# A written order of 1,403 steps replaced by another one, in a fused linear-attention and gated-MLP kernel

## The chip, the cores and the metric

The kernel runs on one core of a Trainium2 chip. The metric is the device time of one execution in microseconds (us), less is better. A core has a matrix engine (PE, which takes its weights through a load stream, PEld), a vector engine (DVE), a scalar engine (ACT), a general engine (POOL), a queue (SP) from which nearly all transfers are issued here, and 16 DMA engines. Each engine takes its instructions in the order in which they were written and waits on semaphores for the others.

## What is computed

For each of 4 batches and 8 heads of width 48, over 768 positions: a state of 48 x 48 decays and collects outer products, and the query reads it. The result x (768 x 384 for each batch) goes through a gated layer.

```python
f = 1.0 / (1.0 + np.exp(-f_logit))
for t in range(S):
    state = f[:, :, t, :, None] * state + np.einsum('bhd,bhe->bhde', k[:, :, t], v[:, :, t])
    y[:, :, t] = np.einsum('bhd,bhde->bhe', q[:, :, t], state)
...
h = np.maximum(x @ w_in, 0.0)
...
    conv_out += conv_w[k][None, None, :] * hp[:, k:k + S, :]
gate = 1.0 / (1.0 + np.exp(-conv_out))
return (h * gate @ w_out).astype(np.float32)
```

w_in is 384 x 1024, w_out 1024 x 384, the convolution has three taps along the positions. The weights come as 64-bit numbers and are made into float32 on the core.

## The kernel before

**Attention.** Positions are cut into 24 chunks of 128 (6 for each batch, numbered 0 to 23). Each chunk goes through: loads F (gates), L (k), M (q), V (v), all issued by SP; x (ACT: exp and ln of the gates); G (sums of them: for chunks 0 to 5 PE, tile pl, L292; later a DVE scan, L297); p (ACT: two exponentials, fi and fd); K (DVE: k scaled, L317 and L320); Q (q scaled, L324: on DVE for chunks 0 to 4, then on POOL); t (POOL: one column of fd). Then the four steps with PE work:

- a, the scores: PE products of k and q into the one PSUM tile pa (L345, from chunk 9 on L351), then a masked copy on DVE (am, L355 and L358).
- k, the transposes: four PE transposes of k into ptk (L330), then a copy on ACT (kp, L333). ptk shares its one PSUM buffer ("s") with pk.
- s, the state: PE products of kp and v into pk (L371, later L376); DVE adds the old state (st, L384); POOL multiplies by the decay (L386).
- y, the values: a first PE visit multiplies scores and v, a second one multiplies q and the state of the chunk before (both py, L398); ACT copies the result into xT (L426) and DVE writes the remainder that the copy's rounding left (L428). xT is thus held as a high and a low half.

**The layer.** A unit is half a batch (384 positions, numbers 0 to 7). Step m*u.f* is one 128-wide slice f of the hidden layer of unit u: three PE visits of three matmuls each (ph, L454: high weights with both halves of xT, low weights with the high half), then relu (L457) and one tap on ACT (L462), two taps on DVE (L464, L466). Step j is tanh on ACT (L473) and the product on DVE (L475). Step r*b.m* is one 128-position slice of the output: the product is split into high and low (gh on ACT, L493; gl on DVE, L495), four PE visits of six matmuls (po, L507), a copy on ACT (L512) and the store. pl, ph and po share three PSUM buffers. The steps c, I, J, H, O, P, S load the weights, make them float32 (POOL, ACT, DVE: L179 to L189) and split them (L192, L195). z, b, h are small ones.

**The order.** Each step is a generator that issues one or a few instructions and yields. `ORDER` (from L26) is a written list of step names; a name that stands there n times is resumed n times. The loop at L573 resumes them one after the other. Nothing else sets the order of any engine's instructions, and a buffer is reused in the order in which the list releases it.

```python
for e in ORDER.split():
    next(todo[e], None)
```

Of the kernel before, what the change touches and what calls it, by code (L numbers as in the profile page):

```python
# [36 lines left out]
P1 j0.2 S5 P2 m1.0 m1.0 p8 S0 F12 Q7 j0.0 a7 h1.0 L9 m1.1 s6 K8 S5 L10 s6 m0.7 Q8 m1.0 a7 y6 k8 P1 P1 m1.2 m0.5 m0.7
m1.3 k8 j0.2 P1 V9 m1.5 m0.6 h1.2 m1.2 m1.2 m0.4 p9 m1.5 m1.3 s7 P2 K9 P4 s7 P1 P4 j0.4 a8 y6 y6 m1.2 P4 P4 S2 m1.3 P1
F13 k9 p9 y7 k9 y7 m1.2 V8 m0.6 m1.4 j0.4 s7 m1.5 a8 m1.7 y7 m1.4 y7 m1.3 m1.4 F14 y8 m1.1 V11 m0.6 m0.7 y8 S1 x12 m1.3
a9 M10 t8 h1.4 L11 m1.5 S2 m1.2 Q9 P4 m1.4 G10 P4 O7 m1.5 P6 P6 a9 s8 j0.6 m1.4 j0.6 y8 S4 y8 h1.6 P6 m1.7 P7 m1.7 m1.2  # L40
s8 P7 m1.6 s8 m1.7 m1.6 M12 m1.6 m1.3 m2.3 p10 m2.3 p10 m2.2 a9 m2.3 m1.6 r0.0 m2.5 m2.2 m1.4 j1.2 L12 K10 r0.1 j1.2
m2.5 m2.2 P6 P6 S1 m2.5 k10 y9 k10 m2.3 m1.5 Q10 S4 a10 s9 m1.7 y9 M13 a10 m2.4 P6 h2.2 P7 P7 S6 m2.2 P7 m2.4 M11 r0.0
t9 r0.0 m1.5 m1.4 S6 j1.4 P7 j1.4 S7 m2.4 S7 m2.5 r0.0 r0.1 m1.1 m1.0 r0.0 y9 r0.0 r0.0 m1.6 r0.1 G11 m1.1 p11 m1.6 r0.1
r0.1 p11 m1.0 m1.0 L13 r0.1 h2.4 t11 m1.6 t10 m1.7 s9 m1.7 m2.4 m2.1 a10 y9 m2.7 r0.1 m2.7 m2.6 r0.2 m2.6 j1.6 j1.0 F15
r0.0 m2.1 r0.2 V10 j1.6 s9 x12 m2.1 Q11 j1.0 K11 G12 m2.7 m2.6 h2.6 m2.4 F17 r0.2 s10 m2.1 r0.5 y10 y10 a11 r0.5 p12 F16
r0.2 m2.6 s10 m2.7 m2.0 h2.0 y10 m2.0 m2.5 m2.0 G14 r0.2 r0.2 x15 m2.4 G13 K12 x15 r0.2 p13 G15 K13 M14 p12 a11 m2.5 p13
s10 r0.5 r0.5 m2.0 r0.1 r0.2 r0.4 m2.2 r0.5 r0.5 V12 m2.1 y10 p14 m2.2 r0.2 r0.4 m2.3 r0.5 m2.2 V13 L14 t12 t13 Q12 Q13
k13 y11 k13 y11 a12 k12 K14 m2.0 m2.6 p15 m2.1 y11 m2.3 r0.2 r0.3 m2.3 m2.1 r0.4 r0.4 y11 m2.5 m2.4 M15 r0.4 r0.4 r0.4
p15 m3.3 r0.4 j2.2 m3.3 m3.2 m3.0 m3.3 k12 a12 V14 a13 y12 m2.0 L15 s12 r0.3 m2.0 j2.4 L16 r0.5 j2.2 m3.0 m3.2 j2.0 m3.0
h3.2 G16 j2.0 a13 y12 m3.2 m2.6 p14 t14 s12 K15 m3.3 m3.1 m3.2 h3.0 m3.1 Q14 j2.4 r0.3 h3.4 r0.3 p16 m2.6 m3.0 m3.1 K16  # L50
F19 m2.7 r0.3 r0.3 m3.1 m2.7 y12 m3.1 L17 m3.4 V16 k14 m2.7 Q15 m3.3 G17 r0.3 r0.3 m3.4 F18 m3.4 m3.7 F20 y13 k14 s13
y13 j2.6 s13 m3.4 y13 y13 a14 k15 p17 j2.6 t15 m3.5 m3.5 r1.0 m3.0 m3.5 K17 m3.5 s13 h3.6 a14 m3.7 m3.7 M18 m3.6 k15
m3.1 m3.6 m3.5 m3.5 s14 y14 L18 y14 M16 r1.0 m3.7 m3.4 s14 a15 r1.1 m3.0 k16 m3.0 p16 m3.4 y14 r1.1 x18 V15 p17 m3.2 x18
m3.6 m3.4 V17 r1.0 r1.0 Q16 L19 V20 y14 a15 m3.6 M17 m3.2 m3.6 m3.7 r1.0 r1.1 Q17 G18 r1.0 r1.0 s14 m3.1 t16 r1.1 r1.1
m3.5 m3.3 m3.3 r1.2 k16 r1.1 m4.4 j3.4 p18 m3.7 r1.1 m3.7 r1.1 s15 y15 y15 M19 m3.6 m3.6 a16 j3.0 j3.4 h4.4 m4.4 s15
m3.2 L23 y15 j3.6 y15 j3.0 m4.4 j3.6 m4.4 j3.2 F22 a16 m4.5 h4.6 m4.6 j3.2 m4.5 m4.6 s15 m4.6 K18 r1.5 m4.7 m4.5 F21 s16
r1.2 r1.2 y16 m4.5 y16 h4.2 y16 p18 a17 s16 r1.2 k18 F23 a17 m4.6 x21 G19 m4.1 m4.5 m4.5 y16 m4.7 m4.7 m4.6 m4.1 m4.1
x21 r1.2 r1.2 m4.1 p19 r1.2 k18 t17 r1.2 Q18 m4.5 m4.6 m4.6 r1.5 K19 s16 m4.7 L20 m4.4 y17 y17 r1.0 m4.4 a18 k19 m4.4
G20 m4.3 r1.2 y17 r1.3 t18 m4.2 p19 p20 m4.2 k19 m4.2 m4.3 a18 m4.7 y17 h4.0 m4.0 j4.4 m4.0 m4.0 m4.7 t19 m4.7 Q19 m4.2
r1.3 m4.3 j4.6 j4.4 m4.1 r1.2 m4.3 V18 m4.1 K20 m4.2 G21 m4.0 m4.0 m4.0 a19 y18 m4.0 M20 s18 j4.6 r1.5 r1.5 y18 y18 r1.5  # L60
r1.5 m4.2 m4.1 s18 h5.4 m5.7 r1.5 j4.0 r1.3 h5.6 m5.6 m5.7 r1.3 m5.7 m4.3 a19 m5.6 m4.2 r1.4 j4.0 r1.3 r1.3 p20 m4.3
m5.7 m4.3 m5.6 r1.3 m5.0 G22 j4.2 m5.3 p21 p21 m5.0 G23 h5.0 m5.0 V19 j4.2 m5.3 s19 y19 s19 y19 Q20 m5.0 r2.1 r1.4 a20
k20 m5.3 r1.5 m5.6 k20 r1.4 m5.0 m5.7 m5.6 L21 h5.2 L22 m5.3 m5.7 K21 r1.4 m5.5 r2.1 M22 m5.5 m5.4 M21 r1.4 y19 r1.4
m5.5 m5.4 r1.4 m5.4 m5.5 a20 m5.4 m5.7 m5.4 V23 t20 m5.2 y19 r2.1 m5.1 m5.6 s19 m5.1 m5.5 t21 r1.4 m5.3 m5.2 m5.1 m5.2
Q21 p23 m5.6 p23 m5.5 K23 k21 m5.1 m5.4 m5.4 y20 k21 s20 V21 m5.5 m5.0 m5.1 r2.0 m5.2 r2.0 m5.0 p22 y20 a21 r2.1 p22
r2.1 m5.1 m5.2 r1.3 y20 m5.3 j5.6 y20 r2.1 t22 m5.2 m5.2 r2.0 r2.0 m5.1 r2.1 m5.3 m6.5 j5.0 r2.0 r2.2 Q22 j5.2 j5.6 r2.0
# [12 lines left out]
"""


# [646 lines left out]
```

## Time and profile before

| | |
|---|---|
| median of 3 runs | 305.28 us (304.31 to 307.17) |
| profiled execution, its own time | 305.0 us |
| its span, first to last instruction | 303.3 us |
| PE busy | 294.2 us (97%), 3747 matmuls and as many weight loads |
| DVE / ACT / POOL busy | 251.3 / 220.5 / 85.3 us |
| transferred | 35.67 MB |
| granted TensorE clock | full from the first slices on |

The span is 1.7 us shorter than the execution's time: that much lies around it. Below, the page's part 1 gives each engine's busy time; the windows give it by stretch; the list of waits says who waited for whom; the chain of waits follows the work that ended last, and where PE stands in it without a break, the length of a piece is what a block of matmuls cost behind the one ahead of it; the timeline shows single instructions.

### The profile page before, as it was taken

Reading aid. Unit: us, or ns where it says so; the run is one execution under the profiler, and the core shown is the slowest. Engines: PE = TensorE matmul, PEld = TensorE weight load, DVE = VectorE, ACT = ScalarE, POOL = GpSimd, SP = SyncE. Lnnn points to the kernel's source line nnn. Section 1 sums busy time; section 2 is a strip of 40 time slices with the busy share of each in tenths; the row PEclk is TensorE's granted clock in tenths of the full one; section 3 lists DMA queues with packets and bytes.
Section 4 is the critical chain, followed back from the end, with each engine's and each line's share of the span. In section 5 each row is a group of like instructions: output and inputs, shape, how many; then the busy total and the mean of one; then the engine's idle time right before and its main releaser. Section 6 shows DMA issues by size and latency. Waiting matters only on the chain.

```text
span 303.3 us, 8894 instructions
## 1 busy us (share of the span) xinstructions
PE 294.2 (97%) x3747; PEld 273.5 (90%) x3747; DVE 251.3 (83%) x380; ACT 220.5 (73%) x422; POOL 85.3 (28%) x107
## 2 busy tenths in 40 slices
...
GB/s 230 396 385 391 403 191 39 56 333 135 2 72 161 101 59 61 220 72 224 102 37 166 64 124 2 195 2 84 3 30 89 2 28 26 28 1 2 79 54 55
DMA packets 19374, 35.67 MB, mean 118 GB/s; under 512 B 2156, under 2 KB 9092, under 8 KB 19332
## 3 DMA queue, kind: packets, MB, share of 16 engines
...
## 4 chain that ended last, share of the span: by engine, by line
PE 75%; DVE 7%; POOL 3%; issue 1%; ACT 1%; POOLq 0%
PE po L507 31%; PE ph L454 28%; PE py L398 8%; PE pa L351 3%; PE ptk L330 2%; DVE g L466 2%; PE pk L376 2%; DVE g L464 2%; DVE g L475 1%; POOL st L386 1%; PE pa L345 1%; DVE am L358 1%; PE pk L371 1%; POOL q L324 1%; DVE gl L495 1%
## 5 line engine op out<-in xcount | busy, mean ns | idle before, releaser
L454 PE MATMUL ph<-xT,wih 128*128 128x384 f32 x384 | 99.6, 340 | 0.0
L454 PEld LDWEIGHTS ph<-xT,wih 128*128 128x128 f32 x384 | 68.3, 188 | 1.0 <-issue 0.2
L507 PE MATMUL po<-woh,gh 128*128 128x384 f32 x192 | 64.7, 337 | 0.0
L454 PE MATMUL ph<-xT,wil 128*128 128x384 f32 x192 | 64.3, 335 | 0.0
L507 PE MATMUL po<-wol,gh 128*128 128x384 f32 x192 | 64.2, 334 | 0.0
L507 PE MATMUL po<-woh,gl 128*128 128x384 f32 x192 | 64.2, 334 | 0.0
L464 DVE SCALAR_TENSOR_TENSOR g<-hb,cw,g 128x384 f32<-128x384 f32 (+1 forms) x64 | 42.2, 667 | 13.0 <-ACT g L462 12.9
L466 DVE SCALAR_TENSOR_TENSOR g<-hb,cw,g 128x384 f32<-128x384 f32 (+1 forms) x64 | 40.5, 649 | 0.7
L457 ACT ACTIVATE hb<-ph 128x384 f32<-128x384 f32 x64 | 30.7, 487 | 11.4 <-PE ph L454 10.8
L495 DVE TENSOR_TENSOR gl<-g,gh 128x1024 fp32r<-128x1024 f32 (+4 forms) x34 | 30.4, 908 | 9.6 <-ACT gh L493 9.6
L462 ACT ACTIVATE g<-hb,cw 128x384 f32<-128x384 f32 (+1 forms) x64 | 38.0, 614 | 0.3
L507 PEld LDWEIGHTS po<-woh,gh 128*128 128x128 f32 x192 | 36.0, 188 | 0.5 <-issue 0.2
L324 POOL TENSOR_TENSOR q<-q,fd 128x512 f32<-128x512 f32 x19 | 26.9, 1419 | 33.0 <-ACT fd L307 24.3
L507 PEld LDWEIGHTS po<-wol,gh 128*128 128x128 f32 x192 | 36.0, 188 | 0.0
L507 PEld LDWEIGHTS po<-woh,gl 128*128 128x128 f32 x192 | 36.0, 188 | 0.0
L454 PEld LDWEIGHTS ph<-xT,wil 128*128 128x128 f32 x192 | 36.0, 188 | 0.0
L493 ACT CAST gh<-g 128x1024 fp32r<-128x1024 f32 (+4 forms) x34 | 26.4, 800 | 12.7 <-PE po L507 8.8
L386 POOL TENSOR_TENSOR st<-st,ft_all 128x256 f32<-128x256 f32 x16 | 20.8, 1301 | 51.7 <-DVE st L384 51.7
L475 DVE SCALAR_TENSOR_TENSOR g<-g,hb 128x768 f32<-128x768 f32 (+1 forms) x32 | 30.1, 952 | 3.7 <-ACT g L473 3.7
L512 ACT COPY ob<-po 128x384 f32<-128x384 f32 x24 | 11.3, 474 | 29.7 <-PE po L507 27.1
L473 ACT ACTIVATE g<-g 128x768 f32<-128x768 f32 (+1 forms) x32 | 26.7, 846 | 3.9 <-DVE g L466 3.8
L312 POOL COPY ft_all<-fd 128x4 f32<-128x4 f32 x24 | 12.7, 537 | 56.5 <-ACT fd L307 56.5
...
## 6 DMA issues: line engine op xcount, KB each, us to landing
k<-in_k_dram SPq DMA_DIRECT2D x24, 256.0 KB, 4.4
q<-in_q_dram SPq DMA_DIRECT2D x24, 256.0 KB, 4.3
...
fb<-in_f_logit_dram SPq DMA_DIRECT2D x18, 256.0 KB, 4.3
...
wos<-in_moe_w_out_dram SPq DMA_DIRECT2D x8, 384.0 KB, 5.6
...
```

Source lines behind the costliest of these rows:

```text
L324: (nc.vector if n < QV else nc.gpsimd).tensor_tensor(raw["q", n], raw["q", n], fds[n][1], ALU.mult)
L398: nc.tensor.matmul(py[G * p:G * p + G, t, :], lhs, rhs, start=start, stop=stop)
L454: nc.tensor.matmul(ph, w, xts[b, hf][:, t, xl, :], start=(k == 0), stop=(k == 3 * KT - 1))
L457: nc.scalar.activation(hb[:, 2:HS + 2], ph, AF.Relu, scale=0.5)
L462: nc.scalar.activation(cv, hb[:, 1:n + 1], AF.Copy, scale=cw[:, 1, f:f + 1])
L464: nc.vector.scalar_tensor_tensor(cv, hb[:, 2:n + 2], cw[:, 2, f:f + 1], cv, ALU.mult, ALU.add)
L466: nc.vector.scalar_tensor_tensor(cv, hb[:, 0:n], cw[:, 0, f:f + 1], cv, ALU.mult, ALU.add)
L473: nc.scalar.activation(cv, cv, AF.Tanh)
L475: nc.vector.scalar_tensor_tensor(cv, cv, 1.0, h_b[:, fp:fp + 2, 1:n + 1], ALU.add, ALU.mult)
L493: nc.scalar.copy(hi, g[:, f:f + k])
L495: nc.vector.tensor_tensor(lo, g[:, f:f + k], hi.bitcast(F32), ALU.subtract)
L507: nc.tensor.matmul(po, g[:, f, :], w, start=(i == 0), stop=(i == 3 * NF - 1))
```

## The change

`ORDER` is written anew. The same 1,403 resumptions stand in it, each step keeps its own sequence, and every engine gets the same instructions with the same operands; only their places change, on PE, DVE, ACT, POOL and on SP's queue. Three lines of each list, where the chunks 3 to 5 are at work:

```diff
...
-s2 P3 H2.1 m0.3 m0.3 k3 t3 P3 K4 a3 J1.1 G6 m0.3 t4 m0.1 m0.1 y3 m0.1 P3 J1.1 y3 P3 m0.3 P0 p5 h0.4 s3 a4 y3 V6 P3 P0 p5
-x8 s3 x8 V4 O5 K5 H0.1 F9 m0.0 O2 a4 m0.0 k4 m0.2 m0.0 P5 Q5 P5 m0.1 k4 m0.2 M6 m0.7 S3 m0.0 m0.1 H1.1 P0 P0 p6 p6 y3 P0
-s3 S3 m0.4 F10 H2.1 m0.2 m0.0 a5 s4 y4 x9 m0.2 y4 P0 P2 H1.1 O4 P2 Q6 y4 G8 O6 a5 L8 m0.7 m0.5 M8 P5 m0.2 P5 s4 m0.7 t6
...
+m0.3 J1.1 O0 p5 F9 m0.3 J1.1 J1.1 V4 Q4 m0.3 K5 J1.1 m0.1 p5 m0.1 s3 P0 O2 G6 s3 P3 P3 m0.3 y3 H1.1 y3 a4 H2.1 y3 k4
+m0.0 x8 L6 s3 P0 H1.1 m0.2 V5 H0.1 y3 m0.2 k4 a4 m0.0 V6 m0.0 P0 p6 m0.2 P3 s4 Q5 h0.4 a5 H0.1 F11 t5 P0 P0 m0.2 y4 y4
+m0.1 m0.0 O5 x8 m0.5 m0.4 P3 H2.1 L9 m0.1 P0 M8 s4 F10 P5 S3 K6 m0.2 t4 P5 m0.0 O7 m0.2 m0.1 P5 y4 m0.4 p6 m0.5 x9 m0.5
...
```

PE's 405 visits (a visit is what one resumption gives PE) stand in 175 stretches of one kind in the old list and in 162 in the new one. How often a kind follows another, counted from the two lists:

| visit, and the one ahead of it | old | new |
|---|---|---|
| ph or po behind pa, pk or py | 12 | 10 |
| ph or po behind ptk | 13 | 14 |
| ph behind po, and po behind ph | 35 | 22 |
| ptk behind ph or po | 6 | 4 |
| pk behind the first visit of py | 5 | 9 |
| first visit of py behind pk (chunk 9 on) | 7 | 3 |
| pa behind the second visit of py | 15 | 9 |
| pa behind pk | 2 | 5 |
| first visit of py behind pa | 3 | 11 |

Other places that are spoken of below:

- POOL: the old list puts one half of P0's conversion, both halves of P5's, t4 and Q5 ahead of the product of the state of chunk 3 (s3); the new one puts them behind it.
- PE: the transposes k4 stand behind two visits of m0.0 in the old list, directly behind the scores a4 in the new one. The set of PE visits ahead of the first visit of m1.1 is the same in both, and so it is ahead of the first visit of r0.1.
- DVE: ahead of the remainder for chunk 2 (y2) the same instructions stand in both lists; ahead of that for chunk 5 (y5) the same but for one (a tap of m0.3 in the old list, the split S0 in the new one); ahead of r0.1's low half the same.
- SP: ahead of the load L7 the new list also has L9, M7, O7, O1 and V5.

## Rows read from the trace of the kernel before

**Rows 1.** The page, part 1: busy us (share of the span) and instructions.

```profile
PE 294.2 (97%) x3747; PEld 273.5 (90%) x3747; DVE 251.3 (83%) x380; ACT 220.5 (73%) x422; POOL 85.3 (28%) x107
```

**Rows 2.** Windows: stretch, length; PE, PEld, DVE, ACT, POOL busy; clock; DMA.

```profile
20.00:30.00 10.00, 9.72 (x179) 8.69 (x172) 10.00 (x17) 9.58 (x23) 5.10 (x6) 1.00 1.02 385
28.00:60.00 32.00, 30.90 (x422) 27.41 (x421) 31.61 (x48) 29.41 (x59) 20.89 (x22) 1.00 0.51 187
```

**Rows 3.** Waits of PE: us in total, times, longest.

```profile
PE py L398 <- POOL st L386: 1.1, 1, 1.1
```

**Rows 4.** The chain of waits: start us, us, what (number of matmuls).

```profile
81.34 0.44 PE ptk L330 x4
81.78 1.01 PE py L398 x32
82.79 0.45 PE pk L376 x32
83.24 0.60 PE py L398 x24
83.83 0.81 PE pa L351 x24
84.65 1.26 PE ph L454 x6
...
99.43 0.58 PE pk L376 x32
100.02 1.47 PE py L398 x56
...
104.10 8.32 PE po L507 x48
...
115.28 0.60 PE ptk L330 x4
```

**Rows 5.** Timeline of POOL: start us, us, line, operation, tiles, shapes.

```profile
34.76 0.71 POOL L181 TENSOR_SCALAR mswo<-mswo 128x384 f32<-128x384 f32 x1
...
38.23 0.89 POOL L181 TENSOR_SCALAR mswo<-mswo 128x384 f32<-128x384 f32 x1
39.08 4.27 POOL L386 TENSOR_TENSOR st<-st,ft_all 128x256 f32<-128x256 f32 x1
...
44.54 1.61 POOL L324 TENSOR_TENSOR q<-q,fd 128x512 f32<-128x512 f32 x1
...
46.72 0.61 POOL L386 TENSOR_TENSOR st<-st,ft_all 128x256 f32<-128x256 f32 x1
```

**Rows 6.** Timeline of PE around two waits and two first visits.

```profile
41.23 1.08 PE L398 MATMUL py<-am,v 128*32 128x128 f32 x32
43.41 0.80 PE L398 MATMUL py<-q,st 128*32 128x128 f32 x24 [1.10 <-POOL st L386]
...
53.10 0.59 PE L454 MATMUL ph<-xT,wih 128*128 128x384 f32 x2
...
90.43 0.33 PE L507 MATMUL po<-woh,gh 128*128 128x384 f32 x1
```

**Rows 7.** Timeline of DVE at the instructions that PE waits for.

```profile
35.02 0.41 DVE L384 TENSOR_TENSOR st<-pk,st 128x256 f32<-128x256 f32 x1
...
44.90 1.80 DVE L317 TENSOR_TENSOR k<-k,fi 128x512 f32<-128x512 f32 x1
...
49.85 0.69 DVE L317 TENSOR_TENSOR k<-k,fi 128x512 f32<-128x512 f32 x1
...
52.29 0.56 DVE L428 TENSOR_TENSOR xT<-py,xT 128x384 fp32r<-128x384 f32 x1 [0.22 <-ACT xT L426]
...
88.76 1.22 DVE L495 TENSOR_TENSOR gl<-g,gh 128x1024 fp32r<-128x1024 f32 x1
```

**Rows 8.** Timeline of SP's queue, and the page's transfers: KB each, us to landing.

```profile
44.31 0.33 SPq L276 DMA_DIRECT2D q<-in_q_dram  x1
...
k<-in_k_dram SPq DMA_DIRECT2D x24, 256.0 KB, 4.4
wos<-in_moe_w_out_dram SPq DMA_DIRECT2D x8, 384.0 KB, 5.6
```

More of the change, by code (lines that the diff above doesn't have):

```diff
@@ L37 @@
[L37 to L66, printed above, removed]
@@ L77 @@
-r3.5 r3.5 r3.3 r3.3 r3.1 r3.3 r3.3 r2.4 r3.4 r3.3 r3.2 r3.2 r3.5 r3.3 r3.4 b r3.5 r3.5 r3.4 r3.4 r3.5 r3.4 r3.5 r3.5
-r3.4 r3.4 r3.4
+F0 x0 I0.0 F1 x0 c G0 x1 p0 x1 p0 M0 L0 J0.0 L1 F2 J0.0 c K0 c J0.0 Q0 I1.0 J0.0 G1 J0.0 J0.0 a0 p1 V0 x2 k0 t0 M1 J1.0
+p1 K1 H0.0 F3 x2 c L2 a0 I2.0 c J1.0 I2.1 Q1 c x3 H0.0 J1.0 J1.0 G2 J1.0 p2 p2 c F7 x3 V1 M2 J1.0 F4 a1 F5 k0 H1.0 y0 y0
+V2 J2.0 J2.0 G3 t1 I0.1 J2.1 a1 y0 s0 K2 J2.1 J2.0 L3 J2.0 y0 M3 c F6 J2.0 s0 c Q2 x7 H1.0 x7 x4 J2.0 y1 y1 p3 k1 t2 x5
+O3 G7 k1 I1.1 x4 a2 L4 p3 k2 G4 a2 k2 s1 J0.1 K3 J0.1 J2.1 x5 M4 s1 J0.1 G5 y1 J2.1 J2.1 s1 y1 Q3 J2.1 p4 H2.0 p4 H2.0
@@ new lines @@
+s2 s2 y2 M6 y2 J0.1 h0.0 L5 V3 t3 J1.1 y2 a3 J0.1 y2 x6 F8 M5 J1.1 J0.1 k3 m0.3 x6 k3 P3 s2 h0.2 m0.1 K4 a3 h0.6 P3 m0.1
+m0.3 J1.1 O0 p5 F9 m0.3 J1.1 J1.1 V4 Q4 m0.3 K5 J1.1 m0.1 p5 m0.1 s3 P0 O2 G6 s3 P3 P3 m0.3 y3 H1.1 y3 a4 H2.1 y3 k4
+m0.0 x8 L6 s3 P0 H1.1 m0.2 V5 H0.1 y3 m0.2 k4 a4 m0.0 V6 m0.0 P0 p6 m0.2 P3 s4 Q5 h0.4 a5 H0.1 F11 t5 P0 P0 m0.2 y4 y4
+m0.1 m0.0 O5 x8 m0.5 m0.4 P3 H2.1 L9 m0.1 P0 M8 s4 F10 P5 S3 K6 m0.2 t4 P5 m0.0 O7 m0.2 m0.1 P5 y4 m0.4 p6 m0.5 x9 m0.5
+M7 O6 Q6 m0.5 m0.4 S3 y4 O4 m0.4 O1 a5 p7 m0.4 m0.6 m0.2 G8 S0 m0.0 P5 a6 s4 y5 L8 t6 y5 k6 p7 L7 S0 m0.5 x9 m0.3 P5
@@ new lines @@
+m0.0 P5 m0.7 K7 P2 m0.7 y5 m0.6 y5 m0.7 V7 k6 p8 m0.7 K8 m0.6 a6 m0.6 P1 G9 k7 j0.0 M10 m0.7 j0.0 m1.1 m0.5 m1.1 m1.0
+m1.0 V8 p9 P2 k7 Q7 m1.1 m1.2 P2 t7 h1.0 P2 m0.3 p8 m0.7 p9 Q8 m1.0 V10 m1.2 S5 m1.1 P2 s6 L10 j0.2 m1.0 a7 s6 y6 a7 k8
+m0.6 m1.2 k8 m0.4 P1 j0.2 m1.3 m1.5 m1.3 m0.4 h1.2 m1.3 m1.2 m0.5 P1 P1 j0.4 P2 K9 s7 a8 P4 P4 s7 k9 y6 F13 m1.5 P4 m1.4
+j0.4 y6 m1.3 S5 y7 y7 P1 m1.4 G10 a8 h1.4 y7 k9 s7 P1 m1.5 M9 a9 m1.5 m0.7 m1.4 Q9 s8 y7 m1.2 F12 P4 P6 t8 m0.6 p10 a9
+m0.6 V9 S2 y8 m1.4 y8 j0.6 m1.6 P4 m1.6 P6 m1.3 S2 P6 P4 m1.6 y8 V13 j0.6 P7 h1.6 m1.7 m1.7 y8 m1.2 m1.6 m1.7 r0.0 S1
@@ new lines @@
+m1.5 p10 S4 m2.2 P6 m2.2 m2.3 m2.3 m2.3 s8 m1.3 m1.7 K10 m1.3 m1.7 t9 m1.2 S1 a9 m1.5 P7 t10 m1.4 m2.2 m2.5 P7 m2.5 m1.4
+a10 j1.2 j1.2 m1.0 P7 m2.5 P6 m1.4 Q10 k10 k10 a10 s8 h2.2 y9 P6 m1.5 r0.0 s9 y9 m2.2 m2.3 r0.1 m2.4 P7 S4 S6 j1.4 y9
+L11 m2.4 S6 P7 j1.4 S7 h2.4 m1.1 S7 m2.4 m2.4 F14 r0.1 L13 m2.5 r0.0 r0.0 m1.0 r0.0 s9 m1.6 r0.0 r0.1 s9 r0.1 r0.1 r0.1
+M12 m2.1 G11 y9 m1.1 p11 r0.0 m2.7 m1.0 m1.7 r0.2 M11 m1.6 m2.7 r0.1 m1.7 x12 m2.7 p11 m2.0 m2.0 K11 m1.1 m1.6 m2.1 m2.0
+r0.1 j1.0 j1.6 x12 a10 j1.0 m2.1 V11 m2.1 j1.6 r0.2 r0.2 m2.5 m2.7 G12 Q11 r0.2 F15 a11 y10 F16 a11 m2.3 m2.4 r0.5 s10
@@ new lines @@
+y10 m2.6 p12 G13 F17 m2.6 h2.6 t11 r0.5 p12 h2.0 r0.2 m2.0 r0.2 m2.6 m2.2 m2.1 y10 Q12 r0.2 L12 K12 r0.2 r0.0 m2.3 r0.5
+s10 p13 G14 r0.4 y10 m2.3 m2.0 r0.5 K13 m2.6 r0.5 m2.2 m2.7 r0.2 x15 m2.2 r0.5 m2.1 M13 r0.4 r0.2 s10 p14 k12 t12 y11
+y11 L15 k12 r0.3 M14 m2.0 a12 y11 m2.1 p13 k13 L14 r0.4 r0.4 k13 r0.4 r0.4 a12 y11 m3.2 x15 r0.5 M15 V12 m3.2 m2.5 j2.2
+r0.3 m2.4 m2.4 p14 m2.6 G15 m2.0 m3.1 j2.2 K14 h3.2 m3.2 m3.2 m2.6 Q13 m3.1 y12 s12 s12 t13 r0.4 j2.0 m2.5 a13 k14 j2.4
+k14 G17 F18 t14 m3.3 j2.4 m3.1 j2.0 F19 h3.0 m3.1 m3.0 m2.7 m2.6 G16 m3.0 m3.2 m3.0 F20 m3.3 m2.7 L16 m3.3 r0.4 p15 a13
@@ new lines @@
+m3.3 r0.3 r0.3 m3.4 r0.5 m3.4 y12 m3.4 m3.3 K15 r0.3 y12 r0.3 x18 j2.6 p15 p16 M16 t15 y13 s13 Q14 j2.6 K16 V14 r0.3
+r1.1 m3.0 h3.4 s13 p16 y13 a14 r1.1 m3.2 s13 k15 t16 y13 a14 m3.6 V16 y13 m3.1 m3.1 m3.5 r0.3 m3.0 m3.6 m3.5 L17 r1.0
+Q16 m3.6 m3.2 m3.5 m3.4 h3.6 k15 x18 y14 Q15 s14 m3.5 m3.4 m3.0 s14 m3.0 m3.4 r1.0 y14 a15 a15 m3.6 m3.5 p17 G18 y14 k16
+m3.7 m3.7 m3.7 m3.1 m3.7 m3.6 s14 V18 y14 r1.1 m3.6 p17 r1.1 r1.0 t17 m3.4 F22 r1.1 m3.7 j3.0 r1.1 r1.0 r1.1 m3.3 m3.3
+m3.5 m3.6 m3.5 F23 j3.4 K17 r1.0 M18 r1.0 L19 m4.7 k16 V15 p18 m4.7 m3.7 m4.5 p18 a16 y15 s15 j3.2 y15 m4.5 m3.7 M17 V17
```

40 lines of the change are left out of this document (23 added, 17 removed).

## The prediction

> **What bounds the kernel now.** I read the page's part 1 first, then the windows, the waits of PE, the chain of waits, and the timelines where PE stood still. PE is busy for 97% of the span [rows 1], and the waits of PE have one place of size after the first 30 us: the second visit of the values of chunk 4 waited for POOL's state product [rows 3]. Everywhere else PE's blocks stand end to end, so the time is the sum of what PE's blocks cost, plus the start, plus that wait, plus the last copy and store. The second thing to see is DVE: it is busy for 10.00 of 10 us while the first chunks are worked on, and for 31.61 of 32 us from 28 to 60 us [rows 2]. In that stretch PE cannot gain more than DVE can follow. The sum is made against the profiled execution, 305.0 us; the median of the runs shown is 305.28, 0.3 above it.
>
> **The sum of PE's blocks.** The instructions are the same, so only a price that depends on the block ahead can change it. The chain gives these prices, from end to end [rows 4]. A visit of po costs 8.32 / 8 = 1.04 us, one of ph half of that, 0.52. Two visits of ph behind the scores took 1.26, that is 0.22 more than 1.04: leaving the small products for the layer costs about 0.2. Four transposes cost 0.44 behind ph and 0.60 behind the scores. The state product costs 0.58 behind ph and 0.45 behind the first visit of the values; that visit costs 1.01 behind the transposes, and 1.47 - 0.60 = 0.87 behind the state product. The scores cost 0.81. With the counts of the two lists: 2 fewer exits without transposes, -2 x 0.2 = -0.4; 2 fewer transposes behind the layer, +2 x 0.16 = +0.3; 4 more state products behind the values, -4 x 0.13 = -0.5; 4 fewer values behind the state product, +4 x 0.14 = +0.6. The 22 instead of 35 changes between ph and po cost nothing: both run at 0.173 us for each matmul. The four sum to 0.0; I take -0.1, since the state products behind the gate sums (one more) are also a little cheaper. Two neighbourhoods are new: scores of chunk 9 and later directly behind a state product (2) or behind transposes (2). Bounds from the nearest rows: 0.14 less, as the values behind the state product, to 0.22 more, as ph behind the scores, so -0.6 to +0.9 for the four; I take 0, since every scores block after another kind that the chain shows costs 0.81.
>
> So "more visits ending in transposes" is worth little by the rows: an exit saves 0.2, and the transposes in it lose 0.16, because they are then no longer behind the layer.
>
> The Trainium skill (TensorEngine Tiling (Array Packing), Key Properties) says that a change of the tiling mode drains TensorE. By that, each of the 13 stretches that the new list has fewer would save one drain, and the sum would be 13 x 0.2 = 2.6 us lower if each cost what the exit shows. The trace agrees only where a block of small products gives way to ph or po; between small kinds rows 4 show cheaper blocks as well as dearer ones.
>
> **The wait of chunk 4.** The first visit of its values ended at 42.31, the second would have ended 0.60 later and ended at 44.21 [rows 4, 6]: 1.3 us lost. Its state product started on POOL at 39.08 and took 4.27, where the next one took 0.61 [rows 5]. Ahead of it stood four instructions that the new list puts behind it, from 34.76 to 39.08. DVE's addition for it ended at 35.43 [rows 7], and in the new list two halves of P3 (about 1 us) go from in front of it and one K (0.6) comes, so it ends at about 35.0. Even if POOL again takes 4.27, the state is there at 39.4, and PE wants it at about 42. The wait goes: -1.3.
>
> What is late next is k4. It needs the "s" buffer that this same DVE addition frees at 35.0, and it now stands directly behind a4, where PE arrives at about 34.6: two visits of m0.0, 1.04 us, that stood between are moved behind it. That gives +0.4; behind it PE's whole queue waits. Bounds: 0 if DVE is a little earlier, 1.0 if the two visits were its whole cover.
>
> **What DVE lets through.** Up to the first visit of m1.1 PE has the same blocks in both lists. It started at 53.10; without the wait and with that of k4 it could start at 53.1 - 1.3 + 0.4 = 52.2. It needs the remainder for chunk 5, which ran on DVE from 52.29 and for which DVE had stood idle 0.22, so DVE was free at 52.07 [rows 7]. The work ahead of it is the same but for a tap (0.53) that becomes a split (0.47): free at 52.0, done at 52.6. The first visit reads the remainder only with its second matmul, so PE goes on at 52.4 instead of 53.1: 0.7 gained, not 0.9. The next place is r0.1: its low half ended on DVE at 89.98 and PE began at 90.43 [rows 6, 7], so 0.45 is spare, with the same instructions ahead of it on DVE. PE can be 0.4 earlier there, and by as much more as DVE stands idle less, at most the 32.00 - 31.61 = 0.4 of its idle time [rows 2]. I take 0.6 of the range 0.4 to 0.8. After that PE has slack everywhere, the last blocks, the copy and the store are the same, and the gain is kept.
>
> **Queues.** SP's list now has M7 ahead of O6, O4, O1, L8, L7 and V7. M7 waited until 44.31, until the values of chunk 4 had freed its buffer [rows 6, 8], and will wait again, now with six loads behind it. The first to be wanted is L7, by the scaling K7 on DVE at about 51. Released at 43, with three O (384 KB) and two k ahead of the others, it lands at about 43 + 5.6 + 2 = 50 or 51 by the times to landing [rows 8]: just covered. If it is late, K7 holds the remainder of chunk 5 behind it on DVE; 1 us late is 1 us of PE. On ACT the gates x9 stand behind F10, which is issued in front of M7. For places that I did not find I add 0.2: bounds 0 and 2, as the largest wait of the old list was 1.3.
>
> **The start.** DVE does the same instructions up to the remainder of chunk 2, without a gap, so the layer cannot begin earlier than 28 us: 0. L0 and M0 change places on SP, which DVE's first scaling may see by 0.2.
>
> Sum: -0.1 (blocks) - 0.6 (what is left of the wait) + 0.2 (new waits) = -0.5, so 305.0 - 0.5 = 304.5 us.
>
> **The rivals.**
> 1. The gain is carried whole. K on DVE took 1.80 at 44.90, while POOL ran a Q from 44.54, and 0.69 at 49.85 [rows 5, 7]. If that clash of 1.1 us does not come again, DVE is no limit and PE keeps the 1.3, plus a few waits of 0.1 to 0.2: 305.0 - 1.7 = 303.3. For it: the Q in question moves. Against it: it can meet another instruction.
> 2. DVE loses time instead: the same mechanism the other way. Six Q (Q5 to Q10) run on POOL while DVE is full. Each that starts just ahead of a two-operand DVE instruction costs 1.1 us. Three clashes more than before cost 3.3; 0.45 are spare at r0.1 and 0.6 of PE's gain go too, so PE ends 3.3 - 0.45 = 2.9 later than before: 307.9. It decides from the point where DVE loses more than 0.9 us over before, because PE's gain and the spare time at r0.1 are then used up. For it: rows 5 and 7 show it once. Against it: one in the stretch, and the same six Q were there.
> 3. The change does nothing: a new wait of 1 us at k4 or K7 takes the place of the old one: 305.0 to 305.6.
> 4. The drain of the skill's rule is real at every change of kind: by the 0.2 of rows 4, 13 x 0.2 = 2.6 and the 0.5 above: 301.9. Against it: the rows price the neighbourhoods, and they cancel.
>
> The Trainium skill (SBUF — State Buffer, Who interferes with whom) says that DVE and GpSimd exclude each other for a whole instruction when a DVE instruction has two SBUF inputs and the GpSimd one reads SBUF, and that who starts first decides. The trace agrees: 4.27 for POOL and 1.80 for DVE on instructions that took 0.61 and 0.69 elsewhere.
>
> **How the numbers follow.** Forecast 0.52, rival 1 0.17, rival 2 0.12, rival 3 0.15, rival 4 0.04. The range from 302.8 to 307.2 leaves out rival 4 and the upper half of rival 2, and holds the bounds of the new neighbourhoods and of unseen waits; the forecast's own range is 303.7 to 305.3. A difference of under about 1% (3 us) can't be told from no change here. Faster by more than that: rival 4, 0.04. Slower: the upper half of rival 2 and unseen waits, 0.08. Within 1%: 0.88.
>
> **What would show it.** No wait of PE for POOL at 43 us; a wait of some tenths at k4 and, if at all, at m1.1; PE's blocks at the prices of rows 4, scores behind a state product at 0.81. Wrong it would be by long K or Q on DVE, by K7 waiting for its load, or by blocks with new prices.

## The result: slower by 1%, and most of the loss lies in the first 30 us

The new list took 308.04 us in the median of four runs (307.19 to 308.76), the old one 304.82 beside it (304.31 to 307.17): ratio 1.0104, 95% interval 1.0070 to 1.0137. The forecast was 304.5, its range ended at 307.2.

A run's mean granted clock was either 0.996 or more, called full clock below, or 0.994 or less, and the runs of the second kind were mostly one to several us longer: three of these four runs of the new list are of the second kind. The profiled execution is the one at full clock; it took 307.19 us with a span of 305.3; before it was 305.0 with 303.3.

The profile after, first the page's part 1 and the windows (stretch, length; busy time of PE, PEld, DVE, ACT, POOL; granted clock; share and GB/s of the DMA engines), as [rows 1, 2]:

```profile
PE 294.5 (96%) x3747; PEld 273.6 (90%) x3747; DVE 251.2 (82%) x380; ACT 220.7 (72%) x422; POOL 83.9 (27%) x107
...
20.00:30.00 10.00, 8.60 (x177) 6.91 (x172) 8.71 (x15) 8.24 (x19) 4.21 (x7) 1.00 0.98 354
28.00:60.00 32.00, 31.06 (x419) 27.33 (x412) 31.33 (x46) 29.55 (x60) 18.99 (x21) 1.00 0.76 262
```

PE is as busy as before (294.5 against 294.2), so its blocks cost about the same. But from 20 to 30 us PE has 8.60 instead of 9.72, and DVE, which had been busy for 10.00 of 10, has 8.71. The waits of PE (total us, times, longest), as [rows 3]:

```profile
PE pl L292 <- ACT fb L271: 2.5, 2, 1.7
PE pw L171 <- POOL st L133: 1.2, 1, 1.2
PE py L398 <- DVE xT L428: 1.1, 1, 1.1
PE pk L371 <- ACT kp L333: 0.7, 1, 0.7
PE py L398 <- DMA v<-in_v_dram: 0.4, 1, 0.4
PE pk L371 <- DVE st L384: 0.3, 1, 0.3
```

The wait for POOL at 43 us is gone, as forecast. In its place stand waits ahead of the layer (all but the fourth). Timelines of PE, DVE, ACT and POOL at the largest of them:

```profile
25.48 0.69 PE L371 MATMUL pk<-v,kp 128*64 128x64 f32 x16 [0.28 <-DVE st L384]
27.25 1.08 PE L398 MATMUL py<-am,v 128*32 128x128 f32 x32 [1.08 <-DVE xT L428]
...
30.36 0.66 PE L454 MATMUL ph<-xT,wih 128*128 128x384 f32 x2
```
```profile
8.59 0.69 DVE L317 TENSOR_TENSOR k<-k,fi 128x512 f32<-128x512 f32 x1 [3.17 <-ACT fb L271]
...
24.40 0.69 DVE L317 TENSOR_TENSOR k<-k,fi 128x512 f32<-128x512 f32 x1 [0.77 <-DMA k<-in_k_dram]
...
26.64 0.56 DVE L428 TENSOR_TENSOR xT<-py,xT 128x384 fp32r<-128x384 f32 x1 [0.53 <-ACT xT L426]
```
```profile
25.60 0.63 ACT L183 ACTIVATE mswi<-mswi 128x512 f32<-128x512 f32 x1 [1.55 <-POOL mswi L181]
26.14 0.46 ACT L426 CAST xT<-py 128x384 fp32r<-128x384 f32 x1
```
```profile
23.82 0.64 POOL L179 TENSOR_SCALAR mswi<-wis 128x512 f32<-128x512 f32 x1 [3.69 <-DMA wis<-in_moe_w_in_dram]
```

The same places in the profile before, PE first:

```profile
27.97 0.69 PE L454 MATMUL ph<-xT,wih 128*128 128x384 f32 x2
```
```profile
7.60 0.69 DVE L317 TENSOR_TENSOR k<-k,fi 128x512 f32<-128x512 f32 x1 [2.17 <-ACT fi L305]
...
20.91 0.66 DVE L317 TENSOR_TENSOR k<-k,fi 128x512 f32<-128x512 f32 x1
...
24.26 0.54 DVE L428 TENSOR_TENSOR xT<-py,xT 128x384 fp32r<-128x384 f32 x1
```

Read it backwards. The values of chunk 2 (27.25) waited for the remainder of chunk 1 on DVE (26.64). Two delays stood ahead of it. K3 had stood 0.77 for the load L3. And ACT's copy came late (0.53), because a weight conversion ahead of it waited 1.55 for POOL, and POOL for the load I0.1. In the old list DVE did the same two instructions, K3 and the remainder, without a gap. By the events at which a transfer's 16 parts landed, L3 was complete at 24.31 (before 20.37) and I0.1 at 23.68 (21.64). The two delays are 1.3 of the 2.4 by which the remainder was late. Another 0.6 was there by the remainder of chunk 0, since DVE's first scaling K0 began 1.0 later: L0 was complete at 8.50 instead of 7.16 (the row of K0 names an instruction of ACT that K0 does not read). The other 0.5 is instructions that took longer. In a second profile of the new list (a2, below) the first 0.6 is gone, and the two delays are 1.01 and 0.53.

The first layer product began at 30.36 instead of 27.97, 2.4 later; the span grew by 2.0. So loads of SP's queue came late. SP's queue (issue, us, what), first after, then before:

```profile
8.51 1.01 SPq L215 DMA_DIRECT2D wis<-in_moe_w_in_dram  x2
13.72 0.33 SPq L259 DMA_DIRECT2D fb<-in_f_logit_dram  x1
14.09 0.43 SPq L281 DMA_DIRECT2D v<-in_v_dram  x1
...
17.77 0.43 SPq L276 DMA_DIRECT2D k<-in_k_dram  x1
```
```profile
9.89 0.33 SPq L281 DMA_DIRECT2D v<-in_v_dram  x1
12.79 0.33 SPq L259 DMA_DIRECT2D fb<-in_f_logit_dram  x1
```

F7 at 13.72 waits until the gate sums of chunk 2 have freed its buffer. In the old list V1 stood ahead of it and was issued at 9.89; now V1 and all behind it wait with it, and L3 also stands behind V2 and I0.1.

### The profile page after: what moved, and what is told of

It is laid out like the page before. It is cut to its first block, busy times and chain, and to the rows that moved or that the text cites. A ratio compares the mean times of both kernels' runs of the same rounds, so it can differ in the third digit from the quotient of the medians.

```text
span 305.3 us, 8881 instructions
## 1 busy us (share of the span) xinstructions
PE 294.5 (96%) x3747; PEld 273.6 (90%) x3747; DVE 251.2 (82%) x380; ACT 220.7 (72%) x422; POOL 83.9 (27%) x107
## 4 chain that ended last, share of the span: by engine, by line
PE 85%; DMA 6%; ACT 3%; SPq 2%; DVE 2%; issue 1%; DVEq 0%; ACTq 0%
PE po L507 33%; PE ph L454 30%; PE py L398 10%; DMA k<-in_k_dram 4%; PE pa L351 4%; PE ptk L330 3%; PE pk L376 2%; PE pa L345 2%; DMA fb<-in_f_logit_dram 2%; PE pk L371 1%; SPq L259 1%; ACT fi L305 1%; SPq L226 0%; DVE am L355 0%; ACT fb L268 0%
## 5 line engine op out<-in xcount | busy, mean ns | idle before, releaser
L464 DVE SCALAR_TENSOR_TENSOR g<-hb,cw,g 128x384 f32<-128x384 f32 (+1 forms) x64 | 41.0, 652 | 18.1 <-ACT g L462 17.9
L466 DVE SCALAR_TENSOR_TENSOR g<-hb,cw,g 128x384 f32<-128x384 f32 (+1 forms) x64 | 39.1, 626 | 0.4
L324 POOL TENSOR_TENSOR q<-q,fd 128x512 f32<-128x512 f32 x19 | 27.6, 1459 | 38.5 <-ACT fd L307 26.7
L495 DVE TENSOR_TENSOR gl<-g,gh 128x1024 fp32r<-128x1024 f32 (+4 forms) x34 | 31.1, 923 | 6.4 <-ACT gh L493 6.4
L386 POOL TENSOR_TENSOR st<-st,ft_all 128x256 f32<-128x256 f32 x16 | 14.1, 882 | 67.0 <-DVE st L384 67.0
L398 PE MATMUL py<-am,v 128*32 128x128 f32 x768 | 25.9, 275 | 1.5 <-DVE xT L428 1.1
L312 POOL COPY ft_all<-fd 128x4 f32<-128x4 f32 x24 | 16.3, 683 | 33.2 <-ACT fd L307 33.2
```

What stands on the lines that cost most here:

```text
L324: (nc.vector if n < QV else nc.gpsimd).tensor_tensor(raw["q", n], raw["q", n], fds[n][1], ALU.mult)
L398: nc.tensor.matmul(py[G * p:G * p + G, t, :], lhs, rhs, start=start, stop=stop)
L464: nc.vector.scalar_tensor_tensor(cv, hb[:, 2:n + 2], cw[:, 2, f:f + 1], cv, ALU.mult, ALU.add)
L466: nc.vector.scalar_tensor_tensor(cv, hb[:, 0:n], cw[:, 0, f:f + 1], cv, ALU.mult, ALU.add)
L495: nc.vector.tensor_tensor(lo, g[:, f:f + k], hi.bitcast(F32), ALU.subtract)
```

## Experiments: the start against the rest, SP against the engines

In all tables the median of the runs at full clock, with their count of all, stands beside the median of all runs. The old list, run beside each group, had 114 of 152 at full clock and 304.3 us in them (304.2 to 304.5 by group). The profiles of q2, u1, u2, t1, t2, t3 and t4 fell on runs at the lower clock, so their first ph lies later than the others' for that reason too. Line numbers in these kernels are 2 lower, since the list takes two lines less (in the three with a product, 1 higher behind it).

| kernel | median us | ratio to the old list | at full clock: us, runs | first ph in its profile |
|---|---|---|---|---|
| s1: old start, new rest | 304.02 | 0.9969 (0.9932 to 1.0006) | 304.0, 11 of 12 | 27.96 |
| s2: new start, old rest | 306.89 | 1.0065 (1.0031 to 1.0099) | 306.5, 4 of 12 | 30.30 |
| q1: new list, old order of first loads | 305.44 | 1.0011 (0.9970 to 1.0053) | 305.4, 9 of 12 | 30.80 |
| q2: old list, new order of first loads | 309.24 | 1.0133 (1.0070 to 1.0196) | 308.2, 1 of 6 | 32.00 |

```diff
 s1: the new list, but ahead of all, in the old list's order:
+F0 I0.0 F1 x0 x0 c L0 M0 G0 x1 I1.0 F2 J0.0 p0 ... V3 h0.6     (162 resumptions)
 q1: SP's queue of the new list
-F0 I0.0 F1 c M0 L0 L1 F2 I1.0 V0 M1 F3 L2 I2.0 I2.1 F7 V1 M2 F4 F5 V2 I0.1 L3 M3 F6 O3 I1.1 ...
+F0 I0.0 F1 c L0 M0 I1.0 F2 L1 L2 M1 F3 V0 I2.0 I2.1 V1 F7 M2 M4 F4 F5 L3 I0.1 L4 V2 M3 I1.1 ...
 s2, q2: the same with the lists exchanged
```

> The new list with the old list's first 162 resumptions (up to the first visit of ph) put in front, on all engines; the other resumptions follow in the new list's order. Theory A (the order of the loads on SP in the first 30 us costs the 2.4 us by which the layer began later) and rival B (the order on ACT and DVE in the same stretch costs it) both expect the first ph at about 28.0 us and 304.3 to 305.5 us. Rival C (the loss lies behind the start, or in a lag of the transfers that has nothing to do with the order) expects 307 to 308.5.

> The old list with the new list's first 158 resumptions put in front; the rest in the old list's order. A and B: the first ph at about 30.4 us and 306.8 to 307.5 us, the old wait for the state of chunk 4 still there or covered by the later start. C: 304.5 to 305.5.

> The new list with the same places for loads, but its first 35 loads (up to O0) in the order in which the old list has them: L0 ahead of M0, V1 ahead of F7, L3 ahead of I0.1, V2 and V0 later. All else is the new list. A: the first ph at about 28 us, 304.8 to 305.8 us. B: first ph at 30 us, 307.5 to 308.3. C: 307 to 308.5.

> The old list with its first 33 loads (up to O0) in the new list's order, all else the old list. A: first ph at about 30 us, 306.5 to 307.5 us. B: first ph at 28 to 28.3, 304.5 to 305.5. C: 304.5 to 305.5.

s1 and s2 settle where: all of the loss comes from the order of the first 160 resumptions, and the new rest is, if anything, better than the old one. Rival C is out. q1 and q2 test which queue. In the medians the loads decide: with the loads alone exchanged the old list loses more than the new list does, and with the loads alone put back the new list comes back to the old one's time.

At full clock the loads explain less. The new list takes 305.7 there (3 runs; 306.0 in f1 below, 12 runs) and s1 304.0; q1, with all its first loads in the old order, is at 305.4. It gets back 0.3 to 0.6 of that difference, and 1.4 is left. And q2, with late loads and the old order on the engines, took more than s2, which has both new (308.2, one run, against 306.5). So the engines' order, rival B, is not out: in these runs either one exchanged alone cost time. What else may stand in q1's 1.4 is one late part: in its profile, which fell on its slowest run at full clock, F7's last part landed 2.5 us behind the other fifteen, and SP stood in the middle of its loads:

```profile
14.46 3.68 SPq L257 DMA_DIRECT2D fb<-in_f_logit_dram  x2
18.18 0.43 SPq L274 DMA_DIRECT2D k<-in_k_dram  x1
```

From 15.10 on, an instruction fetch of 16 KB took 2.68 us in that profile; in most others such a fetch in this stretch took 0.9 to 1.1. It may have held the part back, which is not shown. Four of q1's runs took 304.0 to 304.6, as s1 did. Whether the 1.4 is such a late part or the engines' order stays open.

## Experiments: which loads

| kernel | median us | ratio to the old list | at full clock: us, runs | first ph |
|---|---|---|---|---|
| u1: old list, F7 ahead of V1 | 305.91 | 1.0043 (1.0012 to 1.0073) | 305.6, 6 of 12 | 30.45 |
| u2: old list, L3 behind V2 and I0.1 | 307.05 | 1.0080 (1.0052 to 1.0109) | 306.6, 6 of 12 | 31.39 |
| u3: old list, M0 ahead of L0 | 304.81 | 1.0007 (0.9977 to 1.0037) | 304.5, 8 of 12 | 28.00 |
| t1: new list, V1 ahead of F7 | 306.54 | 1.0067 (1.0041 to 1.0093) | 304.9, 3 of 12 | 29.04 |
| t2: new list, L3 ahead of V2 and I0.1 | 307.08 | 1.0066 (1.0035 to 1.0097) | 306.5, 5 of 11 | 31.41 |
| t3: new list, both | 306.37 | 1.0065 (1.0039 to 1.0090) | 305.5, 4 of 13 | 33.94 |
| t4: new list, V1 ahead of F7, L0 ahead of M0 | 305.76 | 1.0039 (1.0014 to 1.0063) | 305.1, 7 of 12 | 31.19 |

```diff
 u1, SP's queue of the old list          u2
-... I2.1 V1 F7 M2 ...                  -... F4 F5 L3 I0.1 L4 V2 M3 ...
+... I2.1 F7 V1 M2 ...                  +... F4 F5 V2 I0.1 L3 L4 M3 ...
 t1, SP's queue of the new list          t2
-... I2.1 F7 V1 M2 ...                  -... F4 F5 V2 I0.1 L3 M3 ...
+... I2.1 V1 F7 M2 ...                  +... F4 F5 L3 V2 I0.1 M3 ...
```

> The old list with one exchange on SP: F7 ahead of V1. Theory A1 (the stop of SP at F7, with V1 behind it, empties the transfer queues and is the larger part of the loss): first ph at 28.7 to 29.5 us and 305.3 to 306.3. Theory A2 (the places of L3 and I0.1 carry it, the stop is hidden behind I2.1, which is under way until 15.4): first ph at 28.0 to 28.3, 304.3 to 304.9.

> The old list with L3 two places later on SP: V2 and I0.1 (736 KB) go ahead of it. At 400 GB/s it lands 1.8 us later, at 22.2; in the trace of before it landed at 20.37 and its scaling on DVE began at 20.91 without a gap, so 0.54 are spare. A2: DVE stands still for 1.3 us, first ph at 29.0 to 29.5, 305.5 to 306.2. A1 and a theory that only several late loads together cost time: first ph at 28.0 to 28.4, 304.3 to 305.0.

> The old list with one exchange on SP: M0 ahead of L0. L0 then lands at about 7.8 instead of 7.15, K0 began at 7.60 and DVE has no gap behind it: 0.2 to 0.4 us later at the first ph, 304.6 to 304.9. If the first scaling has time to spare: no difference, 304.4.

> The new list with one exchange undone on SP: V1 ahead of F7, as in the old list. Theory A (the places of single loads carry the loss; the exchange alone cost the old list 1.3 us): 0.8 to 1.5 us less than the new list's 307.2 to 308.0, so 306.2 to 307.0, and less of a dip of the transfer rate at 15 to 20 us. Rival (with the other loads still late, DVE meets the next late load and the exchange is worth nothing): 307.2 to 308.

> The new list with L3 put ahead of V2 and I0.1 on SP. It landed at 24.31 with 736 KB less ahead of it that is 22.5, and K3 stands on DVE at about 23.6 to 24.4. Theory A: DVE's wait of 0.77 ahead of K3 goes; but V2 and I0.1 keep their neighbours, and I0.1's conversion (ACT idle 1.55 ahead of it, with the copy of y1 behind) still comes late, so first ph at 29.6 to 30.2 and 306.8 to 307.4. If L3 is the main cause, as in the old list where this cost 2.6 us: 305.0 to 306.0.

> The new list with both: V1 ahead of F7 and L3 ahead of V2 and I0.1. Theory A: the stop of SP at F7 no longer holds V1 and what is behind it, first ph at 28.5 to 29.5, 305.3 to 306.3, close to the list with all its first loads put back (305.4). Rival (the order on the compute engines): 307 to 308.

> The new list with two exchanges undone on SP: V1 ahead of F7 and L0 ahead of M0. With the first alone undone it took 304.9 in runs at full clock and 306.5 in the median. If L0 matters here, where K0 had waited for it until 8.6 and PE stood still for it: another 0.3 to 0.6 less, 304.4 to 304.7 at full clock, and fewer runs at the lower clock. If not: 304.9 and as many.

Against the old list's runs at full clock beside them (304.2), one exchange of two neighbours (u1) costs 1.3 us, and L3 two places later (u2, where V2 and L4 move too) 2.4, more than was expected. So both effects, A1 and A2, are there in the old list, where each load has little to spare. u1, SP's queue: nothing was issued between 9.6 and 14.4, and V1, issued at 9.89 before, waited with F7. This profile was at the lower clock from 8.3 on, and 1.65 of that stop lie behind 12.79, when the old list issued F7.

```profile
7.70 1.90 SPq L213 DMA_DIRECT2D wis<-in_moe_w_in_dram  x2
14.44 0.33 SPq L257 DMA_DIRECT2D fb<-in_f_logit_dram  x1
14.81 1.09 SPq L279 DMA_DIRECT2D v<-in_v_dram  x1
```

u2, the scaling K3 on DVE. 0.54 of the 1.8 by which L3 moves were to spare; the expected standstill was 1.3 and it was 1.54 (the clock was still full there). Why the time lost is larger than the standstill is not shown.

```profile
22.38 0.70 DVE L315 TENSOR_TENSOR k<-k,fi 128x512 f32<-128x512 f32 x1 [1.54 <-DMA k<-in_k_dram]
```

u3, the exchange that the prediction had named, costs nothing that can be told (304.5 against 304.2 at full clock, within the scatter). Taken back one by one in the new list, V1 and F7 give 0.7 us at full clock (t1, against 305.7 for the new list, three runs each; f3 against f1 below shows the same with twelve each) and L3 nothing (t2). Neither gives as much in the median, since t1 has 9 of 12 runs at the lower clock. t3 and t4, at 305.5 and 305.1, are no better than t1, and neither is q1 with all first loads put back. So of the difference between the new list and s1 at full clock 0.7 is traced to one exchange, and the rest to no single load.

## Experiments: the lower clock

The medians of these kernels move by more than their runs at full clock, and most kernels with late loads have fewer of these. So the new list was run again, and then with one more product on PE, which nothing reads, where PE had stood still.

| kernel | median us | ratio to the old list | at full clock: us, runs | first ph |
|---|---|---|---|---|
| a2: new list again | 307.79 | 1.0080 (1.0041 to 1.0119) | 305.3, 2 of 9 | 30.05 |
| f1: new list and one product | 305.96 | 1.0025 (0.9998 to 1.0051) | 306.0, 12 of 12 | 29.70 |
| f3: t1 and one product | 305.23 | 1.0001 (0.9970 to 1.0032) | 305.2, 12 of 12 | 28.13 |
| f2: s1 and one product | 303.96 | 0.9960 (0.9934 to 0.9987) | 304.0, 12 of 12 | 28.77 |
| s1 again | 304.04 | 0.9978 (0.9951 to 1.0006) | 303.9, 9 of 12 | 27.88 |

```diff
 f1, f2, f3: behind the gate sums of chunk 0 in summed()
+            if n == 0:
+                fill = ps.tile([P, NP * HP], F32, tag="mm", name="fill", bufs=MB)
+                nc.tensor.matmul(fill, zr[:, :P], zr, start=True, stop=True)
```

> The new list unchanged, in as many runs as the experiments had, beside them. Theory D (the later loads cost in two ways: the layer starts later, and PE, standing still in the first 30 us, more often loses the full clock there): 306.6 to 307.3 us in the runs with a mean clock of 0.996 or more, which are less than half of the runs, and 308 to 309 in the others; of the old list's 98 runs so far 24 had the lower clock. Theory E (the clock is chance, the order has no part in it): a quarter of the runs or fewer at the lower clock.

> The list with the old start and the new rest once more, to see whether it beats the old list beyond chance: 0.3 to 0.7 us less than the old list in the same session, 303.6 to 304.1 us, and at most a quarter of the runs at the lower clock. If the first result was chance: no difference.

> The new list with one product of zeros (the form of the warm-up's, 0.95 us, its result is not read) put on PE behind the gate sums of chunk 0. Theory F (PE's spell without work before the gate sums of chunk 1 brings the lower clock): at most 4 of 12 runs below 0.996, where the new list had 10 of 13, and a median of 305.5 to 306.3 instead of 307.8. Theory G (another spell, for example that at 24 to 28 us, or chance): 7 or more of 12, median 307 to 308.

> The same product in the new list with V1 back ahead of F7, which had 9 of 12 runs at the lower clock and 304.9 us at full clock. F: at most 4 of 12, median 304.8 to 305.3 instead of 306.5. G: 7 or more, 306 to 307.

> The same product in the list with the old start and the new rest, which had 4 of 24 runs at the lower clock. F: at most 2 of 12, median 303.7 to 304.1. G: no difference beyond chance. If the product delays the gate sums of chunk 1: 0.1 to 0.3 us more.

With the four runs of the first comparison the new list had 3 of 13 at full clock (304.97, 305.65, 307.19); the old one 114 of 152. Theory D had put the new list at 306.6 to 307.3 at full clock: there it lost less than that, and the clock took more. No profile of the new list fell on a run at the lower clock. Where the clock falls, in t4: PE at the gate sums of chunk 1 (timeline), and the windows.

```profile
8.40 1.98 PE L290 MATMUL pl<-tri,fb 128*64 128x128 f32 x16 [2.48 <-ACT fb L269]
...
6.00:8.00 2.00, 0.00 (x0) 0.00 (x0) 0.04 (x1) 1.10 (x3) 1.51 (x4) 1.00 1.03 385
8.00:10.00 2.00, 1.60 (x16) 1.58 (x16) 1.78 (x3) 1.93 (x4) 0.71 (x1) 0.51 1.04 383
10.00:12.00 2.00, 2.00 (x20) 1.70 (x16) 1.55 (x3) 1.58 (x4) 0.93 (x1) 0.50 1.05 395
12.00:14.00 2.00, 2.00 (x14) 1.45 (x14) 1.56 (x2) 2.00 (x6) 0.87 (x2) 0.50 1.05 428
14.00:16.00 2.00, 2.00 (x30) 1.83 (x26) 2.00 (x6) 1.55 (x4) 0.00 (x0) 0.78 0.58 223
```

PE stood for 2.48 us, and behind it the granted clock was 0.5, the lower level of 1.2 GHz, until about 15 us; the 16 products took 1.98 us instead of 1.09. With the one product in that place (f1) PE stood only 1.23, and the clock stayed:

```profile
6.62 0.70 PE L293 MATMUL fill<-st 128*128 128x256 f32 x2
8.54 1.09 PE L290 MATMUL pl<-tri,fb 128*64 128x128 f32 x16 [1.23 <-ACT fb L269]
...
6.00:8.00 2.00, 1.32 (x12) 0.74 (x8) 0.00 (x0) 0.96 (x3) 1.74 (x4) 1.00 1.04 388
8.00:10.00 2.00, 1.21 (x18) 0.97 (x20) 1.47 (x3) 2.00 (x6) 0.33 (x2) 1.00 1.00 368
```

In all 36 runs of the three kernels with the product the clock was full; the same lists without it had 23 of 49 at the lower one (new list 10 of 13, t1 9 of 12, s1 4 of 24). The old list, run beside the three, had 9 of 29 at the lower clock, so the session was not free of it. Theory F is thus shown for this spell. It is not the only one: in u2 it was the standstill at 24 to 26 us behind which the clock fell.

```profile
24.00:26.00 2.00, 0.33 (x10) 0.33 (x12) 2.00 (x4) 2.00 (x5) 0.30 (x1) 1.00 1.01 391
26.00:28.00 2.00, 1.62 (x42) 1.47 (x41) 2.00 (x5) 0.41 (x1) 0.72 (x2) 0.76 1.05 410
28.00:30.00 2.00, 2.00 (x40) 1.24 (x31) 1.54 (x3) 0.42 (x2) 1.92 (x2) 0.50 1.05 405
```

And standing still does not always bring it: s2 and u3 stood 1.80 and 2.39 at the place of t4's standstill in their profiles and kept 1.00, while t1, u1 and t2 fell to 0.50 behind 1.47, 1.78 and 2.00.

In u1, t1, t2 and t4 the clock fell between 8.1 and 9.6 us, before F7 was issued (13.8 to 15.3). So the landings of F7, V1 and L3 cannot have brought it there. F7, which waits for PE's gate sums, was in turn issued later in t1 (13.8) than in f3, the same list with the clock held (13.1). Why these lists lose the clock at this place more often than the old one is not shown. The spell at 24 to 28 us is another matter: in u2 it was the load L3 that DVE and then PE stood for.

The parts of the loss follow. f1 and f2 differ by the order of the start alone, with the clock held: 305.96 - 303.96 = 2.0 us for the new start, its loads and its order on the engines together. Of these, 0.7 are V1 behind F7 (f3 against f1); the other 1.3 are not divided further. f2 against the old list at full clock (304.3 to 304.5): 0.4 to 0.5 less, the new rest. The new list's medians of 307.8 and 308.0 lie 1.8 to 2.0 above f1: the lower clock, in three runs of four. Its runs at the lower clock had 308.7 in the median.

f2 takes as long as s1 (303.96 against 304.02 and 304.04), but no run of it is above 305.3. It is the one kernel whose interval lies below the old list: 0.9960 (0.9934 to 0.9987).

## Experiments: the wait of chunk 4, and DVE in the start

| kernel | median us | ratio to the old list | at full clock: us, runs | first ph |
|---|---|---|---|---|
| u4: old list, s3's product early on POOL | 304.55 | 0.9996 (0.9972 to 1.0020) | 304.5, 9 of 12 | 28.09 |
| x1: s1, scan of chunk 7 late on DVE | 305.30 | 1.0039 (1.0010 to 1.0068) | 304.8, 9 of 12 | 27.68 |

```diff
 u4, POOL's order in the old list        x1, DVE's order in s1
-t4 P0 P0 P5 Q5 P5 s3 P2                 ahead of K3:
+t4 P0 P0 s3 P5 Q5 P5 P2                -G7
                                         behind the remainder of chunk 2 (y2):
                                        +G7
```

> The old list with one change on POOL: the product of the state of chunk 3 goes ahead of both halves of P5 and of Q5. The wait of PE of 1.1 us for it should go. The prediction's theory (DVE lets 0.6 to 0.8 through): 303.6 to 303.9. Rival 1 (carried whole): 303.1 to 303.4. If another engine gives it back: 304.4 to 304.8.

> The list with the old start and the new rest (304.0 us), with one DVE instruction of the start put later: the scan of chunk 7 (1.21 us) goes behind the remainder of chunk 2, which the layer waits for. If DVE's work sets the start of the layer: first ph at 26.9 to 27.3 instead of 27.96, and 302.9 to 303.4 us if DVE keeps up later, 303.5 to 304.0 if it gives the gain back at about 52 us (first visit of m1.1). If transfers set it (V2 landed at 23.3): first ph at 27.7 to 28.0 and no change.

In u4 POOL's product took 0.99 instead of 4.27 [rows 5], and PE's wait of 1.1 [rows 3] is gone:

```profile
35.75 0.99 POOL L384 TENSOR_TENSOR st<-st,ft_all 128x256 f32<-128x256 f32 x1
```

Its profiled span is 0.5 below that of the old list's profile, about what the prediction had let through; but the 12 runs show none of it (at full clock 304.5 against 304.2 for the old list beside it). Whether the product takes 4.27 in most runs of the old list can't be seen: it did in the profiles of before and u3. x1 took 1.21 us of work from in front of what the layer waits for on DVE. The layer began 0.3 earlier, not 0.7 to 1.1. What DVE saved it lost again at the next load: K3 came earlier and now stood 0.97 for L3, where s1 has no such wait:

```profile
20.59 0.69 DVE L315 TENSOR_TENSOR k<-k,fi 128x512 f32<-128x512 f32 x1 [0.97 <-DMA k<-in_k_dram]
```

So the landing of L3, and not DVE's work alone, sets the start even in the old order. And more than the 0.3 was given back where DVE was late (waits of PE in x1, none of which s1 has):

```profile
PE ptk L328 <- DVE st L382: 0.7, 1, 0.7
PE pk L369 <- ACT kp L331: 0.7, 1, 0.7
```

## Where the prediction was right, and the step that failed

**The start: 0.** This step failed, and with it the forecast: in place of 0 the new start cost 2.0 us with the clock held (f1 against f2), and the lower clock came on top. The step's reason, that DVE did the same instructions without a gap, was true of the old list [rows 2] and said nothing of the new one: DVE had no gap because each load came in time. The prediction named a single exchange on SP there (L0 and M0, 0.2). It moved DVE's first scaling by 1.0 in the profile after and by 0.4 in u3, where it cost nothing that can be told. The prediction did not go through the other places: V1 behind F7, L3 behind V2 and I0.1. The profile of before had what was wanted: the time at which F7 was issued, against V1's, and the 0.54 us between L3's landing and K3. From these the standstill of 1.3 us was worked out for u2 before it ran (1.54 measured). That the engines' order of the start has its own part in the 2.0 was not foreseen either; how large it is stays open.

The range ended too low in the same place. No rival had a late load in the start; the late load that one did have (K7, rival 3) ended at 305.6. Rival 2 came near the result with 307.9, but for another reason, more clashes of DVE with POOL: DVE was busy for 251.2 us instead of 251.3, so it is not that. Its point of decision was also off. It takes PE's gain and the spare time at r0.1 as two amounts, 0.9 together, but an earlier PE uses up that same spare time: by its own terms the gain is gone once DVE has lost 0.45.

**What the clock adds.** The sum took the clock as given, since it was full in the one profile [rows 2]. In most runs of the new list it fell: 1.8 to 2.0 us in the median, as much as the new start itself. That the standstill ahead of the gate sums of chunk 1 brings it is shown by the product that keeps it away.

**Blocks: -0.1.** Right as far as can be told: PE's busy time was 0.3 higher, and 0.4 lower in s1. The new neighbourhood that was taken at 0.81, between bounds of 0.67 and 1.03, in the chain of waits of after:

```profile
72.57 0.61 PE pk L371 x16
73.19 0.81 PE pa L351 x24
```

So there is no price of 0.2 on each change of kind, and rival 4 falls: with 13 stretches fewer, PE was busy for 294.5 instead of 294.2, where it wanted 2.6 less.

**The wait of chunk 4.** Right in the profile: it goes, POOL's product took 0.99 from 37.18, and the values follow their first visit without a wait. The new wait at k4 was put at 0.4, and the trace shows 0.1.

**0.6 let through.** s1 is the test, for it has the old start: 0.4 to 0.5 at full clock, 0.3 and 0.2% in the medians, whose intervals include no change. The forecast had 0.5 for the whole, so its size was about right for all but the start. That this gain comes from the wait of chunk 4 is not shown: u4 took away the same wait in the old list and gained nothing. The size may be luck.

**L7 "just covered", 50 to 51.** In s1 it landed at 50.3 and K7 did not wait. In the new list M7 was freed late (44.38 instead of 41.98), L7 landed at 53.25, and K7 stood 0.28 for it:

```profile
53.28 0.94 DVE L317 TENSOR_TENSOR k<-k,fi 128x512 f32<-128x512 f32 x1 [0.28 <-DMA k<-in_k_dram]
```

This was a late effect of the start, not of L7's new place. At 59 us PE stood 0.7 for a copy of ACT that came behind DVE; in that, the next scaling, K8, which took 1.43 instead of 0.76 in s1, weighs more than the load.
